# A new data layout for a fused attention and spectral-gate kernel: whole-batch loads, doubled head blocks, one merged tail of frequencies

## The chip, the cores and the metric

The kernel runs on one core of a Trainium2 chip. The metric is the device time of one launch in microseconds (us). TensorE multiplies matrices; VectorE, ScalarE and GpSimd work on elements, and GpSimd also issues the loads that cast. "Clock" is the share of full speed that the throttle granted TensorE; 1.00 is full.

The record calls an execution slow when it is over 1.5% above the fastest of its kernel. All profiles after the first were taken in fast runs. The profile before was not: its execution, 414.37 us, is 2.0% above the fastest. Where this matters, the profile of run b_tt2 stands beside it (the same kernel but for four buffers in the gate; 409.01 us, fast). The span of a profile is about 2 us shorter than the time of the same execution.

## The reference, cut to what matters

Eight batches. In each, eight heads attend twice: 32 packed rows `p` attend to the keys and values, then the queries attend to the 32 packed results. The 512 columns so made go through a projection to `x1, x2, x3`; `x2` is filtered in the frequency domain, the three are multiplied, and an output matrix follows.

```python
p_packed = sm_attn(p, k, v)              # q, k, v: 8 batches x 8 heads x 576 x 64
out      = sm_attn(q, p_packed, p_packed)
x        = out.transpose(0, 2, 1, 3).reshape(B, S, H * D)
x1, x2, x3 = split(x @ w_proj, 3)        # 512 columns each
x2_conv  = irfft(rfft(x2) * rfft(filter))   # over the 576 rows
y        = (x1 * x2_conv * x3) @ w_out
```

The kernel keeps `out` as a product: the normalised weights of the second attention (`a2n`, 576 x 256) times a small matrix (`qm`, 256 x 1536: packed results times `w_proj`). So the Fourier transform is applied to `a2n`, and the spectrum, its product with the filter and the inverse follow.

## The kernel before

One batch passes through attention, then the gate of the batch before it. Every head has its own load of `k`, `q` and `v`, in rows of 64 values, cast to 16 bits on the way by the queue that GpSimd feeds:

```python
def att_stage1(b):
    for g in range(NPAIR):                       # values, one load per head
        for hh in range(2):
            nc.gpsimd.dma_start(v_ring[:, rv, :, 0:D],
                vflat[base:base + NT * P, :].rearrange("(i tl) d -> tl i d", tl=P))
    for g in range(NPAIR):                       # pairs of heads
        ...                                      # p: load, transpose, two copies
        for ti, (tensor_f, nm) in enumerate(((kflat, "k"), (qflat, "q"))):
            for hh in range(2):
                nc.gpsimd.dma_start(stt[:, :, hh, :], tensor_f[base:base + NT * P, :]...)
            # 5 transposes, 2 copies
        # 5 score matmuls, 2 exponentials
```

Normalising the second attention took 20 small multiplies per batch on VectorE (160 of them in the trace). The spectral product works on frequency tiles of 128, 128 and 33; the third costs as much as a full one (0.68 us a multiply against 0.69, 1.27 us each on GpSimd for both):

```python
for m in range(3):                               # 128, 128, 33 frequencies
    # fre, fim: spectrum of this tile (4 matmuls)
    nc.vector.tensor_tensor(out=tt1, in0=fre, in1=hre_sb[.., m, :], op=ALU.mult)
    nc.vector.tensor_tensor(out=tt2, in0=fim, in1=him_sb[.., m, :], op=ALU.mult)
    nc.vector.tensor_tensor(out=tt3, in0=fre, in1=him_sb[.., m, :], op=ALU.mult)
    nc.vector.tensor_tensor(out=tt4, in0=fim, in1=hre_sb[.., m, :], op=ALU.mult)
    nc.gpsimd.tensor_tensor(out=outre, in0=tt1, in1=tt2, op=ALU.subtract)
    nc.gpsimd.tensor_tensor(out=outim, in0=tt3, in1=tt4, op=ALU.add)
```

Program order: loads and keys of batch 0, weights, filter, rest of batch 0; then attention of batch b, gate of batch b-1. In the trace TensorE's matmuls follow this order.

The softmax here doesn't subtract the row's maximum and nothing guards it: scores larger than these inputs give would overflow.

## Time and profile before

| | before |
|---|---|
| median time | 408.25 us (406.24 to 414.37, 4 runs) |
| start, to the first key transposes of batch 1 | 70.4 us |
| first period | 47.9 us |
| steady period (mean of six) | 44.4 us: attention 24.0, gate 20.2 |
| last gate, last store | 24.0 and 4.2 us |
| busy: TensorE, VectorE, GpSimd | 333.9, 240.6, 228.2 of 412.6 us |

Read it by stages: the shares over the whole run hide that the start is short of data, that attention runs at a clock of 0.72, and that the gate waits for a product made on VectorE and GpSimd. The profiled execution was the slowest of its four (414.37 us). In the profile of b_tt2 the steady period is the same (44.3 us), but the start is 66.0 us and the first period 47.4. The lines themselves are in the prediction.

### The profile page before, as it was taken

How to read it: one execution, taken by the hardware profiler on the slowest of the kernel's cores; microseconds unless marked ns; L12 is line 12 of the kernel's file. 1: busy time of each engine (PE TensorE's matmuls, PEld its weight loads, DVE VectorE, ACT ScalarE, POOL GpSimd, SP SyncE). 2: the span in 40 equal slices, each digit the busy share in tenths (PEclk: the TensorE clock that was granted, in tenths of full speed). 3: DMA queues.
4: the chain of work that ended last, by engine and by line, in shares of the span. 5: the costliest groups of instructions: out<-in, count | busy, mean ns of one | idle time of the engine just before them, and what ended most of it. 6: DMA issues, size and time to landing. Idle time of an engine off the chain costs nothing.

```text
span 412.6 us, 6577 instructions
## 1 busy us (share of the span) xinstructions
PE 333.9 (81%) x2220; PEld 186.6 (45%) x2220; DVE 240.6 (58%) x832; ACT 159.9 (39%) x436; POOL 228.2 (55%) x247
## 2 busy tenths in 40 slices
PE   0365798768897979798998899798979798889985
PEld 0242214434554446544563365436544366436452
DVE  2246116474856485667656584748555855758382
ACT  1011137345253715271346325452527143632323
POOL 8868301993449571996189536956397704043160
PEclk9999958659995899669985989588967997599999
DMA  9999901994069902991199409980499026000303
GB/s 200 182 208 210 227 2 10 87 86 26 1 141 103 71 1 105 108 95 7 53 138 97 30 2 162 98 55 2 127 106 81 2 76 75 0 2 0 116 0 116
DMA packets 138226, 33.05 MB, mean 80 GB/s; under 512 B 129552, under 2 KB 130960, under 8 KB 138192
## 3 DMA queue, kind: packets, MB, share of 16 engines
q0 software_dynamic: 125808, 15.72, 61.1%
q1 hardware_dynamic: 8096, 10.06, 7.4%
q10 hardware_dynamic: 4288, 6.85, 5.7%
q8 instruction: 17, 0.28, 0.3%
q14 instruction: 17, 0.14, 0.1%
HBM read 38.88 MB, written 9.44 MB: 117 GB/s over the span
## 4 chain that ended last, share of the span: by engine, by line
PE 50%; POOL 10%; DVE 9%; DMA 5%; issue 4%; POOLq 0%; ACT 0%; ACTq 0%; DVEq 0%
PE ops_b L392 9%; PE qps_b_g L298 8%; PE x2c_b L370 7%; PE fa2ps_b L318 6%; POOL gfull_b L350 5%; PE s_b_g L262 4%; DVE tt_b L341 4%; PE misc_b_g L253 3%; DMA qst_b_g<-in_q_dram 3%; DVE zrec_b_g L256 3%; PE x_b L376 2%; PE x_b L374 2%; PE trps_b_g L227 2%; PE a2tp_b L309 2%; POOL gtail_b L350 2%
## 5 line engine op out<-in xcount | busy, mean ns | idle before, releaser
L222 POOL DMA_DIRECT2D kst_b_g<-in_k_dram x63 | 55.5, 888 | 70.4 <-PE misc_b_g L207 53.2
L198 POOL DMA_DIRECT2D v_ring<-in_v_dram x63 | 55.4, 886 | 27.1 <-PE misc_b_g L253 24.9
L379 ACT COPY x1sb_b<-x_b 128x288 f32<-128x288 f32 x64 | 25.6, 399 | 98.3 <-PE x_b L374 70.4
L350 POOL TENSOR_TENSOR gfull_b<-tt_b,tt_b 128x512 f16<-128x512 f32 x16 | 20.3, 1268 | 69.6 <-DVE tt_b L341 69.6
L222 POOL DMA_DIRECT2D qst_b_g<-in_q_dram x63 | 55.7, 892 | 1.3 <-DMA v_ring<-in_v_dram 1.3
L370 PE MATMUL x2c_b<-afull_sb,gfull_b 128*128 128x288 f16 x256 | 45.7, 299 | 8.9 <-POOL gfull_b L350 8.7
L299 ACT CAST q_sb_b<-qps_b_g 64x512 f16<-64x512 f32 x96 | 49.4, 579 | 0.6
L298 PE MATMUL qps_b_g<-wp_sb,pp_ring 128*64 128x512 f16 x96 | 39.3, 594 | 0.0
L256 DVE RECIPROCAL zrec_b_g<-misc_b_g 64x32 f32<-64x32 f32 x64 | 19.5, 333 | 31.0 <-PE misc_b_g L253 30.8
L253 PE MATMUL misc_b_g<-e_b_g,v_ring 128*128 128x64 f16 (+1 forms) x320 | 32.5, 225 | 6.3 <-DVE pp_ring L257 4.7
L229 DVE COPY kT_b_g<-trps_b_g 128x512 f16<-128x512 f16 x32 | 13.6, 425 | 40.6 <-PE trps_b_g L227 39.3
L392 PE MATMUL ops_b<-wout_sb,yt_b 128*128 128x512 f16 (+1 forms) x160 | 36.8, 380 | 0.0
L340 DVE TENSOR_TENSOR tt_b<-fre_b,hre_sb 128x512 f32<-128x512 f32 (+1 forms) x24 | 16.5, 689 | 32.9 <-PE fre_b L333 29.7
L376 PE MATMUL x_b<-a2t_b,q_sb_b 128*128 128x288 f16 x128 | 32.6, 287 | 3.9 <-ACT x1sb_b L379 3.9
L370 PEld LDWEIGHTS <-gfull_b 128*128 128x128 f16 x256 | 24.7, 101 | 23.6 <-POOL gfull_b L350 15.5
L374 PE MATMUL x_b<-a2t_b,q_sb_b 128*128 128x288 f16 x128 | 31.5, 290 | 1.9 <-ACT x1sb_b L379 1.9
L262 PE MATMUL s_b_g<-pp_ring,qT_b_g 128*128 128x64 f16 (+1 forms) x160 | 18.0, 238 | 16.3 <-DVE pp_ring L257 16.3
L395 ACT ACTIVATE osb_b<-ops_b 128x512 f32<-128x512 f32 (+1 forms) x40 | 23.8, 596 | 17.6 <-PE ops_b L392 8.9
L382 DVE SCALAR_TENSOR_TENSOR yt_b<-wtmp_b,x2c_b 128x288 f16<-128x288 f32 x64 | 26.9, 451 | 6.3 <-PE x2c_b L370 5.5
L381 DVE TENSOR_TENSOR wtmp_b<-x1sb_b,x_b 128x288 f32<-128x288 f32 x64 | 27.6, 447 | 4.9 <-ACT x1sb_b L379 4.4
L237 ACT ACTIVATE e_b_g<-misc_b_g 128x256 f16<-128x256 f32 x32 | 12.3, 383 | 43.0 <-PE misc_b_g L234 43.0
L253 PEld LDWEIGHTS <-v_ring 128*128 128x128 f16 (+1 forms) x320 | 21.1, 111 | 15.0 <-issue 6.6
(73 smaller groups left out, 586.5 us busy)
## 6 DMA issues: line engine op xcount, KB each, us to landing
out_dram<-osb_b SPq DMA_DIRECT2D x32, 256.0 KB, 2.1
v_ring<-in_v_dram POOLq DMA_DIRECT2D x63, 80.0 KB, 3.3
kst_b_g<-in_k_dram POOLq DMA_DIRECT2D x63, 80.0 KB, 3.3
qst_b_g<-in_q_dram POOLq DMA_DIRECT2D x63, 80.0 KB, 3.4
wpst<-in_moe_w_proj_dram ACTq DMA_DIRECT2D x12, 256.0 KB, 5.3
wost<-in_moe_w_out_dram ACTq DMA_DIRECT2D x4, 256.0 KB, 4.6
fst<-in_moe_filter_fft_dram ACTq DMA_DIRECT2D x4, 256.0 KB, 6.0
out_dram<-osb_b SPq DMA_DIRECT2D x8, 128.0 KB, 2.6
```

What stands on the lines that cost most here:

```text
L198: nc.gpsimd.dma_start(v_ring[:, rv, :, 0:D], vflat[base:base + NT * P, :].rearrange("(i tl) d -> tl i d", tl=P))
L222: nc.gpsimd.dma_start(stt[:, :, hh, :], tensor_f[base:base + NT * P, :].rearrange("(i tl) d -> tl i d", tl=P))
L253: nc.tensor.matmul(ppz, v_ring[0:tsz[i], rv, i, :], e1[0:tsz[i], i, :], start=(i == 0), stop=(i == NT - 1))
L256: nc.vector.reciprocal(zrec[:], ppzp[D:D2, hh, hh * NPK:(hh + 1) * NPK])
L262: nc.tensor.matmul(s2ps[0:tsz[i], i, :], qT[:, i * P:i * P + tsz[i]], pp_ring[:, g, :], start=True, stop=True)
L298: nc.tensor.matmul(qps[:], pp_ring[:, g, :], wp_sb[:, g, ts(c, 512)], start=True, stop=True)
L299: nc.scalar.copy(out=q_sb[r0:r0 + 2 * NPK, g // 2, ts(c, 512)], in_=qps[:])
L350: nc.gpsimd.tensor_tensor(out=outre, in0=tt1[0:nf, :], in1=tt2[0:nf, :], op=ALU.subtract)
L370: nc.tensor.matmul(x2c[:], lhs, rhs, start=(j == 0), stop=(j == nk - 1))
L374: nc.tensor.matmul(x1[:], q_sb[:, ht, ts(m, P)], a2t_sb[ht][:, c0:c0 + cn], start=(ht == 0), stop=(ht == 1))
L376: nc.tensor.matmul(x3[:], q_sb[:, ht, ds(2 * DM + m * P, P)], a2t_sb[ht][:, c0:c0 + cn], start=(ht == 0), stop=(ht == 1))
L392: nc.tensor.matmul(ops[0:tsz[i], :], yt_sb[:, m, i * P:i * P + tsz[i]], wout_sb[:, m, :], start=(m == 0), stop=(m == ND - 1))
```

## The change

Its intent: fewer, longer transfers; fewer, larger instructions; a shorter spectral product. The diff, cut to its core (`...` marks cuts):

```diff
-            nc.gpsimd.dma_start(v_ring[:, rv, :, 0:D], vflat[...])            # 24 loads per batch
-                    nc.gpsimd.dma_start(stt[:, :, hh, :], tensor_f[...])
+        nc.gpsimd.dma_start(kn[:], k[b].rearrange("h (p i) d -> p h (i d)", i=KI))   # rows of 1.5 KB
+        nc.gpsimd.dma_start(vn[:], v[b].rearrange("h (p i) d -> p h (i d)", i=KI))
+        nc.gpsimd.dma_start(qn[:], q[b, :, 0:512, :].rearrange("h (p i) d -> p h (i d)", i=4))  # 1 KB
+        nc.gpsimd.dma_start(qt[0:32, :, :], tail[0])
+        nc.gpsimd.dma_start(qt[32:64, :, :], tail[1])
...
+    rings = [const.tile([P, H, 2 * NPK], FP16, ...)]      # doubled blocks: two heads side by side
+        for t in range(2):                                # p times v for four heads at once
+            for i in range(KI):
+                nc.tensor.matmul(pv[:, t, :], e1[:, i, ts(t, P)], vn[:, 4 * t:4 * t + 4, ts(i, D)], ...)
+                nc.tensor.matmul(z1[:, t:t + 1], e1[:, i, ts(t, P)], ones[0:KP, :], ...)
...
-                nc.vector.tensor_tensor(out=a2n[0:tsz[i], i, ...], in0=..., in1=zb, op=ALU.mult)   # x20
+            nc.gpsimd.tensor_tensor(out=a2n[0:n, i0:i0 + w, :]..., op=ALU.mult)                     # x3
...
+        for c in (1, 0, 2):                               # projection: pairs in two halves of the output
+            for t in range(2):
+                for u in range(2):
+                    nc.tensor.matmul(qp[u * D:(u + 1) * D, :], Rd[:, g, NPK:3 * NPK], wp[:, g, ts(c, DM)], ...)
...
-        for m in range(NFT):                              # 3 tiles, 4 multiplies and 2 sums each
+        for m in range(2):                                # 2 such tiles, temporaries with bufs=2
+        ft = spectrum(4)                                  # merged tail: one multiply
+        nc.vector.tensor_tensor(out=gm[:, 4, :], in0=ft[:], in1=htail[:], op=ALU.mult)
...
+    pack_p(0, 1, "a"); prologue_filter(); att1(0); ...    # filter first, forward transform in attention
```

The merged tail: the 33 frequencies left over lie in one tile of 128 rows, real parts twice and imaginary parts twice. One multiply with a filter tile laid out to match gives all four products, and the inverse matmuls form their sum and difference.

## The prediction

> **What bounds the kernel now.** I read the busy shares first, then the 40 slices, then the chain of waits in order of time, and last a table of stages whose borders I took from that chain.
>
> ```profile
> PE 333.9 (81%) x2220; PEld 186.6 (45%) x2220; DVE 240.6 (58%) x832; ACT 159.9 (39%) x436; POOL 228.2 (55%) x247
> ...
> PE   0365798768897979798998899798979798889985
> ...
> PEclk9999958659995899669985989588967997599999
> DMA  9999901994069902991199409980499026000303
> ...
> q0 software_dynamic: 125808, 15.72, 61.1%
> ```
>
> No engine is full. TensorE is the busiest, but its row dips at the start and, once per batch, its clock falls to half. The transfers saturate the first 50 us and then come in bursts. One queue carries nearly all of the cost: 15.72 MB in 125808 packets, 125 bytes each.
>
> The chain of waits ends each batch with the 20 output matmuls. Two of these, 118.27 and 162.47, are one steady period of 44.2 us apart. I cut that period where the spectrum matmuls begin:
>
> ```profile
> 0.00:70.40 70.40, 40.08 (x197) 17.50 (x197) 25.53 (x89) 16.30 (x44) 38.47 (x48) 0.90 1.22 152
> ...
> 118.30:142.30 24.00, 21.21 (x166) 12.63 (x166) 14.33 (x72) 13.42 (x41) 20.83 (x24) 0.72 1.38 108
> 142.30:162.50 20.20, 17.45 (x106) 9.70 (x105) 14.16 (x29) 5.92 (x13) 7.52 (x6) 1.00 0.09 34
> ```
>
> Columns: window, length, busy time and count of TensorE, its weight loads, VectorE, ScalarE, GpSimd, then clock, DMA share, GB/s. So there are four pieces: a prologue of 70.4 us (to the first key transposes of the second batch), seven periods (the first one 47.9 us, it still fills up; six of about 44.3), the gate stage of the last batch (24.0 us), and 4.2 us for the last store. Their sum is 412.6 us. Attention takes 24.0 us of a period at clock 0.72, the spectral gate 20.2 us at full clock.
>
> ```profile
> 133.43 4.71 PE qps_b_g L298 x12
> ...
> 150.16 1.20 POOL gtail_b L350
> 151.50 1.27 POOL gtail_b L351
> 152.82 0.66 PE x2c_b L370 x4
> ...
> 158.04 4.43 PE ops_b L392 x20
> ```
>
> From the chain: in attention the bound is TensorE's program order with short dependent steps at half clock (12 projection matmuls of 512 columns take 4.71 us, 0.39 each; the 20 output ones at full clock take 4.43, 0.22 each). In the gate it is the spectral product, VectorE then GpSimd, whose tail lands at 152.8, 10.5 us after the stage began. Loads appear on the chain, but in 118.3 to 125.9 the same table has TensorE busy 6.85 of 7.6 us with other heads, so that wait hides little.
>
> **What the Trainium skill says.**
> 1. "DMA: Bandwidth & Descriptors", Specifications: transfers under 512 B do not reach line rate. The trace agrees: 129552 of 138226 packets are under 512 B and they make up the saturated prologue. An engine's packet costs 0.611 x 412.6 x 16 / 125808 = 32 ns.
> 2. "TensorE: Matmul & The Clock Gate", Part 1: TensorE runs at half clock until it has been busy for a window of about 3.4 us, and falls back after an idle one. The trace agrees: clock 0.52 in 125.9 to 138.1, full again 4.9 us into the dense projection.
> 3. The same page, Part 3: matmuls whose outputs start in different column groups can run concurrently. No row of this trace has such a pair; the new projection does.
> 4. "VectorE: DVE Perf Modes", Two Vector instructions with no wait between them: an instruction whose operands start in another quadrant is held until the earlier one is done. Agrees: two reciprocals take 0.57 us, hardly less than twice one (0.33).
>
> **The change, part by part.**
>
> *Loads.* Per batch 24 loads become 5. Rows of 256 B in HBM become 1536 B (k, v), 1024 B (q) and 256 B (q tail). GpSimd spent 0.89 us on each old load, 24 x 0.89 = 21.3 us per batch. The new ones have 3072 rows; at 0.89 us per 640 rows that is 4.3 us. On the DMA engines the old rows cost 15360 x 32 ns / 16 = 31 us per batch. For the new ones I take 75 ns per 1.5 KB (estimate: the two hardware queues, with mean packets of 1.2 and 1.6 KB, took 60 and 88 ns per packet by the same division), 55 ns per 1 KB, 32 ns for the tail: (1536 x 75 + 1024 x 55 + 512 x 32) / 16 = 11.7 us. In steady state neither was on the path for long; this pays in the prologue.
>
> *Prologue.* The order of instructions puts the filter first, before any attention; its 2 MB now come on two uncontended hardware queues in rows of 4 to 6 KB. Filter and constants landed: about 9 us. 50 filter matmuls of 512 columns: 9 cold at 0.43 (spacing seen at 40 us) and 41 at 0.2165 (spacing seen at 43 us), 12.8 us, plus 5 x 0.2 us for the 64-row tile (20 old forward matmuls of 289 columns took 3.31 us where 0.122 each makes 2.44: 0.2 more for each of four groups that end in 64 rows): 23 us. Attention of batch 0, from the steps below, 25 us, plus 28 transposes for the rest of p (0.10 each, cold) and their copies, about 4: 52 us. Constants, load 0, the rest of p (1792 rows x 32 ns / 16), weights (1536 x 80 / 16) and load 1 need about 9 + 11.7 + 3.6 + 7.7 + 11.7 = 44 us of DMA, so they just keep ahead. Against 70.4 and the slow first period (47.9 - 44.3 = 3.6): **22 us saved**.
>
> *Attention of a period*, on TensorE in the order that the build gives. Old: 24.0.
> - Keys: per pair of heads 6 transposes (0.50, from 4 in 0.40), copy (VectorE 0.46, ScalarE 0.65: old 512 columns 0.43 and 0.58 scaled), 6 score matmuls (0.33), handovers 0.08. The next pair's transposes stand behind these scores, so nothing overlaps: 1.5 us warm, 1.9 cold; four pairs with the first 5 us warm and ScalarE's exponentials in front of its copies: 6.5.
> - p times v: 12 matmuls of 256 columns and 12 of one column, cold: 12 x 0.213 + 12 x 0.10 = 3.8.
> - Normalisation: drain 0.2, reciprocal 0.2, four multiplies in four quadrants, held, 4 x 0.29: 1.65. Nothing stands in TensorE's order in front of the transposes that wait for it.
> - Transposes of p and q (24 x 0.10) and two copies of 1024 columns (0.70 each), then 20 score matmuls: 4.4.
> - Projection: 12 x 0.427 cold = 5.1, or half if the pairs overlap. But the normalised weights go over GpSimd, 1.27 us for 512 columns: exp 0.6, reduce 0.64, reciprocal 0.2, then 1.27 + 1.27 + 0.7, ready 4.2 us after the scores end. So overlap saves under 2 us.
> - Forward transform 10 x 0.2165 + 0.4, tail 10 x 0.06 + 0.4, transposes 0.95: 4.5.
> Sum 6.5 + 3.8 + 1.65 + 4.4 + 5.1 + 4.5 = 26.0 serial, 24.3 overlapped; I take **25.0, one more than before**. Some 56 small VectorE instructions per batch vanish (40 multiplies of 0.21 us among them), but they ran beside TensorE and pay nothing here.
>
> *Gate.* The merged tail replaces four multiplies of 0.68 by one and two GpSimd operations of 1.27 by none; doubled temporaries remove the 0.2 us stalls. First multiply at 1.07 us, eight at 0.605: end 6.0; GpSimd's four end at 7.45 instead of 10.5. Fewer inverse matmuls fit ahead of it (about 17 of 72 instead of 31, as banks are freed by those multiplies): 55 x 0.122 = 6.7, then 4.43: **18.6 instead of 20.2**.
>
> Period: 25.0 + 18.6 = 43.6 against 44.3, so 7 x 0.7 = 5 us. The last gate does not repeat the forward transform: 18.6 against 24.0, but that work is only moved into the prologue's 52. Total 52 + 7 x 43.6 + 18.6 + 4.2 = 380 us in a profiled run; times 409.05 / 412.6: **377 us**.
>
> **The rivals.**
> - *TensorE stays warm through attention.* Then the steps fall to about 21 us (keys 6.2, p times v 2.0, projection hidden by GpSimd): 7 x 4 = 28 us less, 350. For it: fewer switches to 64-row tiles, a denser p times v. Against: the old attention was busy 21.2 of 24 us by this count and still fell to 0.52; the new one has longer gaps.
> - *The undivided key, normalisation and query steps cost more than I allow*, as all heads now wait together where the old order filled one pair's wait with another pair's transposes. Attention 28: 398 us, about 3% faster. For it: the program order, and every new copy being larger. Against: fewer instructions.
> - *The prologue is bound by casting transfers.* If long rows cost as much per byte as the short ones (32 ns per 256 B), each load takes 28 us and the weights 24: prologue near 90, total 415, slower. Against: the 2 KB rows above, and 32 ns looks like a cost per packet.
> - *GpSimd becomes the bound*: 4.3 + 3.2 + 5.1 = 13 us per period: no.
>
> **Range and chances.** Steps of attention are uncertain by 2 us, times 7, the prologue by 6, the gate by 1, times 8: together about 18. I take 353 to 398 for 8 in 10. The limit of 2% is 401 us; only the second rival at its worst or the third one reach it: faster 0.90, same 0.07, slower 0.03.
>
> **What would show it.** The first key transposes of the second batch near 52 us; DMA share of the software queue near 20 to 25%; output matmuls 43.6 us apart; the window of attention near 25 us with a clock still near 0.7; the last spectral product on GpSimd about 7.5 us after the spectrum begins; gate 18.6. Wrong it would be if periods are under 40 (warm clock) or over 46 (serial steps), or if the prologue does not shrink.

## The result, and the profile after

| | before | predicted | after |
|---|---|---|---|
| time | 408.25 us | 377 (353 to 398) | 357.59 us (356.74 to 358.35, 4 runs) |
| start | 70.4 | 52 | 53.3 |
| first period | 47.9 | 43.6 | 41.4 |
| steady period | 44.4 | 43.6 | 39.9 |
| attention / gate | 24.0 / 20.2 | 25.0 / 18.6 | 21.6 / 18.0 |
| last gate / store | 24.0 / 4.2 | 18.6 / 4.2 | 17.9 / 3.7 |

The ratio is 0.875 (95% interval 0.870 to 0.879): the changed kernel is faster. The record notes no check of its result, but calls runs that leave its arithmetic alone (a_short, a_serialproj) correct. The periods are the distances between the starts of the output matmuls of neighbouring batches. Of the 56.8 us between the two profiled spans, the start gives 17.1, the first period 6.5, the six steady ones 26.7 and the end 6.6. Against the fast profile of b_tt2 (span 407.0) they are 12.7, 6.0, 26.5 and 6.0: some 4.4 us of the 17.1 are the slow execution, not the change.

The page of the changed kernel: busy times, then 40 slices of the span (TensorE, its clock, transfers), then the software queue (packets, MB, share).

```profile
PE 281.9 (79%) x2162; PEld 170.7 (48%) x2162; DVE 161.6 (45%) x376; ACT 127.1 (36%) x259; POOL 94.7 (27%) x106
...
PE   0596777789868896789777896789778896889995
...
PEclk9997675699958998599959998699968997599999
DMA  7999961940369004920378014930300012000303
...
q0 software_dynamic: 29408, 16.52, 35.2%
```

TensorE lost 52 us of busy time, VectorE 79 and GpSimd 134, yet the row of the clock still has one dip per batch, as before. The packets fell to less than a quarter, the share of the queue only to 35.2%: a packet now costs 0.352 x 355.8 x 16 / 29408 = 68 ns instead of 32.

The same table of stages as in the prediction: start, one attention, one gate.

```profile
0.00:53.30 53.30, 33.47 (x240) 16.92 (x240) 15.58 (x35) 15.98 (x29) 18.53 (x28) 0.86 1.16 196
...
134.50:156.10 21.60, 16.54 (x160) 10.82 (x159) 6.78 (x19) 9.36 (x19) 6.25 (x8) 0.76 0.72 108
156.10:174.10 18.00, 16.58 (x106) 9.62 (x106) 12.31 (x27) 5.57 (x12) 4.95 (x4) 1.00 0.11 38
```

Attention has TensorE busy 16.5 of 21.6 us at clock 0.76; the gate is at full clock. The chain of waits, in order of time, for the start and for one period (start, length, what):

```profile
1.26 10.56 DMA pnat<-in_p_dram
...
13.69 13.52 PE hp L204 x49
...
135.48 0.47 PE s_b L226 x6
...
135.97 0.49 ACT e_b L228
136.46 0.54 ACT kT_b L222
...
143.19 0.28 DVE ppn_b L245
...
151.18 1.05 POOL a2n_b L295
...
152.28 2.25 PE fp_b L320 x8
...
160.74 1.23 POOL gm_b L359
...
170.11 3.96 PE o_b L396 x17
```

In the start, a small load of `p` lands at 11.86 us and the filter's matmuls follow; they end at 27.2. In a period the chain hops in the key stage from the scores (`s_b`) to ScalarE's exponential and copy of the next keys (`kT_b`), goes through VectorE's normalisation (`ppn_b`), GpSimd's weights (`a2n_b`), the transform (`fp_b`), GpSimd's product (`gm_b`) and the output matmuls (`o_b`). So TensorE's dependent steps still set attention; no load is on the path of a period.

### The profile page after: what moved, and what is told of

Read it like the earlier page. It is cut to its first block, busy times and chain, and to the rows that moved or that the text cites. A ratio compares the mean times of both kernels' runs of the same rounds, so it can differ in the third digit from the quotient of the medians.

```text
span 355.8 us, 5499 instructions
## 1 busy us (share of the span) xinstructions
PE 281.9 (79%) x2162; PEld 170.7 (48%) x2162; DVE 161.6 (45%) x376; ACT 127.1 (36%) x259; POOL 94.7 (27%) x106
## 3 DMA queue, kind: packets, MB, share of 16 engines
q0 software_dynamic: 29408, 16.52, 35.2%
q10 hardware_dynamic: 288, 1.56, 1.1%
## 4 chain that ended last, share of the span: by engine, by line
PE 61%; DVE 14%; POOL 11%; ACT 6%; issue 3%; DMA 3%; POOLq 0%; DVEq 0%; ACTq 0%
PE x_b L381 11%; PE o_b L396 10%; PE pv_b L235 6%; POOL gm_b L359 6%; PE fp_b L320 5%; PE s_b L226 5%; PE hp L204 4%; PE qTp_b L268 4%; DVE zs_b L291 3%; DMA pnat<-in_p_dram 3%; POOL gm_b L360 3%; PE x_b L378 3%; PE x_b L376 3%; DVE ppn_b L245 3%; ACT kT_b L222 3%
## 5 line engine op out<-in xcount | busy, mean ns | idle before, releaser
L381 PE MATMUL x_b<-ac,gm_b 128*128 128x288 f16 x320 | 51.2, 287 | 6.1 <-POOL gm_b L359 5.0
L383 ACT COPY x1s_b<-x_b 128x288 f32<-128x288 f32 x64 | 25.5, 398 | 80.0 <-PE x_b L376 59.8
L381 PEld LDWEIGHTS <-gm_b 128*128 128x128 f16 x320 | 30.0, 98 | 19.9 <-POOL gm_b L359 10.9
L396 PE MATMUL o_b<-wout,y_b 128*128 128x512 f16 (+1 forms) x160 | 38.2, 381 | 0.3
L226 PE MATMUL s_b<-pk,kT_b 128*96 128x64 f16 x192 | 17.1, 232 | 21.9 <-ACT kT_b L222 13.0
L320 PE MATMUL fp_b<-wc,a2n_b 128*128 128x512 f16 (+1 forms) x80 | 24.0, 400 | 11.7 <-ACT qm_b L309 8.5
L398 ACT ACTIVATE os_b<-o_b 128x512 f32<-128x512 f32 (+1 forms) x40 | 23.8, 596 | 22.1 <-PE o_b L396 22.1
L386 DVE SCALAR_TENSOR_TENSOR y_b<-w_b,x_b 128x288 f16<-128x288 f32 x64 | 26.8, 449 | 7.2 <-PE x_b L381 5.5
L385 DVE TENSOR_TENSOR w_b<-x1s_b,x_b 128x288 f32<-128x288 f32 x64 | 27.4, 448 | 4.5 <-ACT x1s_b L383 3.8
L378 PE MATMUL x_b<-a2t_b,qm_b 128*128 128x288 f16 x128 | 26.1, 286 | 3.9 <-ACT x1s_b L383 3.9
L376 PE MATMUL x_b<-a2t_b,qm_b 128*128 128x288 f16 x128 | 26.1, 286 | 1.0
L309 ACT CAST qm_b<-qp_b 128x512 f16<-128x512 f32 x48 | 24.0, 606 | 0.0
```

The source lines that it names most:

```text
L226: nc.tensor.matmul(s1[:, hh, 2 * ii:2 * ii + 2, :], kT[:, hh, ii, :], pk[:, b, 2 * g + hh, :], start=True, stop=True)
L309: nc.scalar.copy(out=qm[:, t, ts(c, DM)], in_=qp[:])
L320: nc.tensor.matmul(fp[:], a2n[0:n, i, ts(t, P)], wc[0:n, i, 0:DM], start=(i == 0), stop=(i == 4))
L376: nc.tensor.matmul(x1[:], qm[:, t, ts(m, P)], a2t[:, t, cols], start=(t == 0), stop=(t == 1))
L378: nc.tensor.matmul(x3[:], qm[:, t, ds(2 * DM + m * P, P)], a2t[:, t, cols], start=(t == 0), stop=(t == 1))
L381: nc.tensor.matmul(x2[:], gm[:, j, ts(m, P)], ac[:, j, cols], start=(j == 0), stop=(j == 4))
```

## The experiments

All were run against the kernel before; each was timed in three rounds. The edits are cut to what matters. Periods are means of six, from the profiles. "Start" is to the first output matmuls of batch 0 (113.7 us before, 89.9 after), or to the key transposes of batch 1 where said (70.4 and 53.3).

### Does the new layout pay through its rows? (no_load, short rows, one load per head)

**Before, loads of batches 1 to 7 removed.**

```diff
-        for g in range(NPAIR):            # loads of k, q, v
+        for g in range(NPAIR if b == 0 else 0):   # batch 0 only, its tiles are kept
```

> The kernel before, but keys, queries and values are loaded for batch 0 only and used again by the other seven batches (wrong result on purpose); TensorE's work is unchanged and the 21 us of descriptor writing per batch on GpSimd are gone. Theory of the prediction (old loads cost the start and the first period, and hide in the steady periods): steady periods stay at 43.5 to 44.5 us, the start shrinks by at most some 5 us because batch 1 no longer queues up behind the rest, total 395 to 408 us. Rival (the old loads also held up the steady attention, which is where its 2.4 us per batch were lost, and the new layout won by being easier on the DMA engines): attention falls by 2 us or more per batch, periods near 42 us, total 380 to 392 us.

Measured 394.99 us (before in these rounds 410.01), ratio 0.959 (0.950 to 0.969), wrong result. The steady period is 43.2 us instead of 44.4, the start 100.5 instead of 113.7. The loads were worth 1.2 us per batch, a bit more than allowed for and less than the rival needs. The start by its profile fell by 13 us, against 5 expected; but 7 x 1.2 = 8.4 of the 15.0 us between the medians leave only 6.6 for it, and the run with two temporaries (below) shows the old start scattering by 5 us with no cause. Against that run's fast profile the first outputs came 8.1 us sooner, and the keys of batch 1 at 58.7 instead of 66.0. What in the loads costs the 1.2 us stays open: the last steady period of the old kernel, with 6 loads left of 24, is no shorter than the others (44.56 us; 44.36 in b_tt2).

**After, keys and values in rows of 256 B.**

```diff
-        nc.gpsimd.dma_start(kn[:], k[b].rearrange("h (p i) d -> p h (i d)", i=KI))
+        nc.gpsimd.dma_start(kn.rearrange("p h (i d) -> p h i d", d=D), k[b].rearrange("h (i p) d -> p h i d", i=KI))
```

> The changed kernel with keys and values loaded in rows of 256 B instead of 1536 B, still one load per tensor and batch, same result. Packets of the software queue go from 29 to about 90 thousand. Theory (the row length is what pays in the start): DMA work per batch rises from some 12 to about 25 us, the second batch's key transposes move from 53 to 58 to 66 us, and since GpSimd must also write 9216 instead of 1536 rows per batch (some 3.6 us more of issue), the period grows by 0 to 2 us: total 363 to 382 us. Rival (the start shortened by order and fewer issues on GpSimd alone, row length does nothing): start within 1 us of 53.3, total within 3 us of 357.6.

Measured 354.77 us (354.03 to 355.10), correct. The queue's line of the page, and the group of key loads on GpSimd (count, busy, mean ns):

```profile
q0 software_dynamic: 90848, 16.52, 64.3%
...
L142 POOL DMA_DIRECT2D kn_b<-in_k_dram x8 | 14.3, 1792 | 76.9 <-PE kTp_b L217 73.2
```

Three times the packets and nearly twice the share of the DMA engines, and no time lost: batch 1's keys start at 51.5 us, the period is 39.95. The theory falls; the long rows of keys and values (1.5 KB) pay nothing here. The queries kept their rows of 1 KB in this run and the next, so those were not tested.

**After, the same short rows, one load per head.**

```diff
-        nc.gpsimd.dma_start(kn[:], ...)   # and vn, qn: 3 loads
+        for h in range(H):                # 24 loads
+            nc.gpsimd.dma_start(kn[:, h, :]..., k[b, h]...)
+            nc.gpsimd.dma_start(vn[:, h, :]..., v[b, h]...)
+            nc.gpsimd.dma_start(qn[:, h, :], q[b, h, 0:512, :]...)
```

> The changed kernel with keys and values in rows of 256 B and with one load per head, so 24 loads and two tails per batch as before the change, some 20 us of descriptor writing on GpSimd per batch instead of 3.6; same result. Rows of 256 B alone changed nothing, because the issue on GpSimd stayed short. Theory (the number of issues on GpSimd is what made the old start long): batch 1's key transposes move from 53 to 60 us or later, and the first output matmuls from 90 to over 97; steady periods 40 to 42 as GpSimd is free for only some 23 us before the next weights need it: total 365 to 385 us. Rival (the start is TensorE's program order, loads are early enough in any form): start within 2 us, periods as before, total within 4 us of 357.6.

Measured 385.42 us (383.17 to 387.56), correct: 30.7 us more than with the same rows of keys and values in whole-batch loads. Batch 1's keys start at 59.4, the first outputs at 102.4, the period is 42.8. Key loads on GpSimd, the chain in the start, and the wait that TensorE's list of instructions shows there:

```profile
L143 POOL DMA_DIRECT2D kn_b<-in_k_dram x64 | 48.1, 754 | 64.2 <-PE kTp_b L218 62.2
```

```profile
47.70 0.72 POOL vn_b L144
48.42 0.43 POOL qn_b L145
...
50.96 1.10 POOL a2n_b L296
...
52.10 4.93 PE fp_b L321 x10
```

```profile
52.10 4.93 PE L321 MATMUL fp_b<-wc,a2n_b 128*128 128x512 f16 x10 [7.75 <-POOL a2n_b L296]
```

GpSimd writes the loads of batch 1 from 27.5 to 50 us. Before 37.7 it stands 5.3 us in three places, by its list for transfers of the projection weights to land; from there on it writes without a pause. The weights of batch 0, which stand behind these loads in its order, come late; TensorE stands 7.75 us. The four steady periods in which such loads are issued take 43.4 to 45.1 us, the two after the last load 40.3 and 40.0, as in the changed kernel. So in this kernel the number of loads that GpSimd has to issue counts, not the rows of keys and values. A load of 576 rows holds GpSimd for 0.754 us, one of 4608 rows for 1.792: by these two, an estimate of 0.6 us per load and 0.26 ns per row. It gives 0.81 us for the changed kernel's key loads of 768 rows (0.805 measured), but 0.77 for the old ones of 640 (0.89 measured).

The 30.7 us are not the share of the gain that fewer loads brought. In the old kernel all loads of seven batches were worth 15.0 us; in the new one they cost more, because the normalised weights now wait behind them on GpSimd.

### The gate: doubled temporaries or merged tail?

**Before, two buffers for each temporary.**

```diff
-            tt1 = sbB.tile([P, DM], FP32, tag="tt1", ..., bufs=1)   # likewise tt2 to tt4
+            tt1 = sbB.tile([P, DM], FP32, tag="tt1", ..., bufs=2)
```

> The kernel before with two buffers instead of one for each of the four temporaries of the spectral product, nothing else. Theory: this is a small share of the gate's gain (the stalls of about 0.2 us at each of two reuses): 0.3 to 0.6 us per batch, total 403 to 407 us. Rival (the waits on the single temporaries were the main part of the gate's 2.2 us): 1.5 us or more per batch, total below 397 us.

Measured 407.92 us against 410.01, ratio 0.990 (0.980 to 1.000): not to be told from nothing. The period is 44.33 instead of 44.36. The whole of the 5 us between the two profiles lies ahead of the first output matmuls (108.7 against 113.7), where the edit does nothing: that is scatter of the old start. The theory's 0.3 to 0.6 us per batch is not there. VectorE's stalls did go (0.26 and 0.16 us in the batch of the prediction), and the last product came 0.4 us sooner after the first multiply, but the period did not follow.

**After, the cost of the unmerged tail put back.**

```diff
-        nc.vector.tensor_tensor(out=gm[:, 4, :], in0=ft[:], in1=htail[:], op=ALU.mult)
+        for j in range(4):
+            nc.vector.tensor_tensor(out=tt[j][:], in0=ft[:], in1=htail[:], op=ALU.mult)
+        nc.gpsimd.tensor_tensor(out=gm[0:64, 4, :], in0=tt[0][0:64, :], in1=tt[1][0:64, :], op=ALU.subtract)
+        nc.gpsimd.tensor_tensor(out=gm[64:128, 4, :], in0=tt[2][64:128, :], in1=tt[3][64:128, :], op=ALU.add)
```

> The changed kernel with the cost of the unmerged tail put back in the spectral product: four multiplies on VectorE and two operations on GpSimd for it instead of one multiply (wrong result on purpose). Two buffers for the temporaries did nothing in the kernel before, so the merged tail should be nearly the whole gain of the gate. Theory: three more multiplies of 0.69 and two more GpSimd operations of about 1.2 us at the end of the chain; the last product lands 3 us later, TensorE covers a part with other matmuls, the gate goes from 18.0 to about 20 us: total 370 to 376 us. Rival (the gate gained by its transposes and forward transform having left it, and the tail is covered): gate under 18.6, total under 362 us.

Measured 369.44 us (368.67 to 371.73), wrong result. The period is 41.8 instead of 39.9, a gate 19.8 instead of 18.0. TensorE's list shows the wait that came back, for the last product:

```profile
166.78 1.03 PE L385 MATMUL x_b<-ac,gm_b 128*128 128x288 f16 x7 [0.97 <-POOL gm_b L366]
```

The merged tail is 1.8 of the gate's 2.2 us, as the theory had it.

### The projection's pairs

**After, another order, so that neighbours mostly write the same half.**

```diff
-            for t in range(2):
-                for u in range(2):            # halves 0, 1, 0, 1, ...
+            for u in ((0, 1) if c != 0 else (1, 0)):
+                for t in range(2):            # halves 0, 0, 1, 1, 1, 1, 0, 0, ...
```

> The changed kernel with its 12 projection matmuls in another order, so that most neighbours write the same half of the output partitions and can't run beside each other; same instructions, same result. If neighbours in different halves do run concurrently (12 in 2.66 us at half clock, where 12 x 0.427 would be 5.1), they now take 4 to 5 us. As GpSimd's normalised weights arrive only 4.1 us after the projection begins, the period grows by 0.5 to 1.5 us and the total by 4 to 11 us, to 362 to 369 us. Rival (the short time comes from the trace's modelled ends, not from concurrency): no change in projection or total, within 1 us.

Measured 357.04 us (355.85 to 359.00), period 40.05, correct. A miss: at half clock a pair of these matmuls takes 0.43 us, against 0.42 in the order before, so the order of neighbours is not what makes them fast. (All 12 take 1.5 to 2.9 us in either kernel, by where the clock rises, so single batches can't be compared.) It did not show that they run side by side, nor that they don't.

**After, all 12 into one half.**

```diff
-                    nc.tensor.matmul(qp[u * D:(u + 1) * D, :], ...)
+                    nc.tensor.matmul(qp[0:D, :], ...)      # the copy takes qp[0:D] alone, qm is zeroed once
```

> The changed kernel with all 12 projection matmuls of a batch writing the lower half of the output partitions, one over the other (wrong result on purpose; the copies take that half alone). The run with another order left the pace as it was, 12 in 2.4 us, so order is not what makes them overlap; this one leaves no second column group to overlap with. Theory (two column groups work side by side, each through its own six): 12 now take 4.7 to 5.1 us at half clock instead of 2.8, the forward transform starts 1 to 2 us later, periods 40.7 to 41.7 us, total 363 to 371 us. Rival (64-column weights simply run at this pace, or the next wait hides it): projection under 3 us or period within 0.4 us of 39.9, total within 3 us of 357.6.

Measured 356.03 us (355.74 to 356.65), wrong result, period 40.15. TensorE's list, first the changed kernel's 11 (a twelfth starts 0.15 us earlier), then this run's 12:

```profile
148.23 2.66 PE L307 MATMUL qp_b<-wp,ppk 128*64 128x512 f16 x11
```

```profile
146.40 4.10 PE L310 MATMUL qp_b<-wp,ppk 128*64 128x512 f16 x12
```

Both parties were half right. Two halves do work side by side: by the starts in the trace, a pair takes 0.42 us at half clock and 0.22 at full with them, 0.86 and 0.43 without. And it pays nothing: in the changed kernel the transform behind the projection then waits for ScalarE's copies and GpSimd's weights, here for nothing. These are the changed kernel's two waits:

```profile
151.27 0.60 PE L320 MATMUL fp_b<-wc,a2n_b 128*128 128x512 f16 x2 [0.37 <-ACT qm_b L309]
152.28 2.25 PE L320 MATMUL fp_b<-wc,a2n_b 128*128 128x512 f16 x8 [0.41 <-POOL a2n_b L295]
```

From the first projection matmul to the end of these ten it takes 6.4 us, the run with one half 6.6.

### Attention's waits and the clock

**Weights normalised on VectorE instead of GpSimd.**

```diff
-            nc.gpsimd.tensor_tensor(out=a2n[0:n, i0:i0 + w, :]...
+            nc.vector.tensor_tensor(out=a2n[0:n, i0:i0 + w, :]...
```

> The changed kernel with the normalisation of the attention weights multiplied on VectorE instead of GpSimd. Same result. Theory (with overlapping projection pairs the transform waits for GpSimd, by 0.4 us, and otherwise for ScalarE's six copies of the projection): gains only about 0.4 us per batch, total 353 to 357 us. Rival (GpSimd sets the end of attention): the transform starts 1 us or more sooner, total 346 to 351 us.

Measured 346.99 us (345.54 to 348.28), correct; period 39.0, 0.9 less. Nearer to the rival: GpSimd, busy for 27% of the run, was on the path all the same, by the place of its work. Six periods give 5.4 of the 10.6 us; the rest lies ahead of the first outputs (84.9 against 89.9), and part of that may be scatter (the keys of batch 1 start at 50.1 here, at 53.3 in the changed kernel, but at 51.1 in a_tail6, which leaves everything before them alone).

**Query transposes ahead of the wait for the normalised heads.**

```diff
+        # in att1, in front of the normalisation: 20 query transposes, copies on ScalarE
-        # in att2: the same transposes, copies on VectorE
```

> The changed kernel with the transposes of the queries placed in TensorE's order before the wait of 1.5 us for the normalised packed heads, which they don't need; two of their copies go to ScalarE so that VectorE is free for the normalisation. Same result. Theory (that wait is idle time on the path): the transposes, 2.1 us at half clock, fill it; attention falls by 1 to 1.6 us and the total by 8 to 12 us, to 345 to 350 us. Rival (the later wait for GpSimd's normalised weights or the queue on ScalarE swallows it): total within 3 us of 357.6.

Measured 359.55 us (357.13 to 361.12), correct: nothing gained, the period is 40.9. TensorE's list behind the scores:

```profile
146.37 1.46 PE L308 MATMUL qp_b<-wp,ppk 128*64 128x512 f16 x11
149.50 0.61 PE L321 MATMUL fp_b<-wc,a2n_b 128*128 128x512 f16 x2 [1.67 <-POOL a2n_b L296]
150.51 3.54 PE L321 MATMUL fp_b<-wc,a2n_b 128*128 128x512 f16 x8 [0.40 <-POOL a2n_b L296]
```

The wait of 1.5 us was filled, the clock came back early and the projection ran at full speed (1.46 us instead of 2.66). Then TensorE stood 1.67 us for GpSimd's weights, the clock fell a second time, and the eight transform matmuls took 3.54 us instead of 2.25. The half clock had only moved to costlier work.

**Key transposes two pairs ahead of the scores.**

```diff
+        kTs = {g: keys(g) for g in range(2)}         # transposes and copy of two pairs
         for g in range(H // 2):
+            kT = kTs.pop(g)
             # 6 score matmuls of pair g
+            if g + 2 < H // 2:
+                kTs[g + 2] = keys(g + 2)
```

> The changed kernel with the key transposes running two pairs of heads ahead of the scores, so that TensorE doesn't stand for each copy. Same result. The prediction counted 'nothing overlaps' here; the trace shows four waits of 0.55 and 0.85 us, 2.8 us per batch. Theory (these waits are on the path): the first wait stays, the other three vanish or nearly: attention falls by 1.5 to 2.2 us, total by 12 to 17 us, to 341 to 346 us. Rival (ScalarE's exponentials and copies bound this stage, 1.2 us per pair of heads with a ScalarE copy): falls by under 0.8 us, total 351 to 356 us.

Measured 321.20 us (319.58 to 324.68), correct; period 35.8, 4.1 less. The clock over 40 slices, and the stages of one batch (attention, gate):

```profile
PEclk9999989799979999899979997899979997899999
```

```profile
118.80:136.40 17.60, 14.25 (x160) 9.28 (x160) 6.72 (x19) 9.36 (x19) 6.25 (x8) 0.90 0.86 134
136.40:154.30 17.90, 16.48 (x104) 9.53 (x104) 12.28 (x27) 5.58 (x12) 4.96 (x4) 1.00 0.10 37
```

The four waits of the key stage shrank from 2.8 to 0.64 us, as expected, but attention fell by 4.0. The other half goes with the clock: it now falls only behind the normalisation's wait, so p times v and its sums take 1.8 us instead of 2.8.

**Useless matmuls in the idle spots.**

```diff
+            fill(b, 2)     # behind each pair's key transposes: 512 columns each, result unused
+        fill(b, 6)         # in the normalisation's wait; 3 behind the query transposes,
+                           # 4 behind the projection
```

> The changed kernel with 21 useless matmuls of 512 columns per batch in TensorE's idle spots of attention (2 behind each pair's key transposes, 6 in the wait for the normalised heads, 3 behind the query transposes, 4 behind the projection); result unchanged. This is the first rival of the prediction, made to happen: if the idle spots are what sends the clock to half, the clock of attention rises from 0.76 to 0.95 or more; p times v falls from 2.75 to 1.4 us, queries and scores from 3.8 to about 2.5, with the fillers costing up to 1 us where they overrun their spots: total 340 to 356 us. Rival (the clock falls whatever TensorE does in this stretch): clock stays near 0.76, and the fillers only add, some 2 to 4 us per batch: total 370 us or more.

Measured 336.64 us (336.11 to 337.56), correct; period 37.7. The stages of one batch:

```profile
125.00:144.75 19.75, 17.42 (x180) 9.83 (x180) 6.68 (x19) 9.36 (x19) 6.24 (x8) 1.00 0.76 120
144.75:162.70 17.95, 16.52 (x104) 9.56 (x104) 12.32 (x27) 5.57 (x12) 4.96 (x4) 1.00 0.10 35
```

Twenty-one matmuls of 0.22 us more per batch made it 21 us faster. The clock is 1.00 throughout, p times v and its sums take 1.8 us. The rival falls: the idle spots are what sends the clock down.

**The three edits together.** Keys ahead, queries ahead, weights on VectorE.

> The changed kernel with three edits together: key transposes two pairs ahead (321.2 us alone), query transposes before the normalisation's wait (359.6 alone, because the half clock then came later, in the transform), normalised weights on VectorE (347.0 alone). Same result. Theory (what the wait costs is mostly the half clock that it causes, and with all three gone nothing sends it down): mean clock 0.97 or more, attention 15 to 15.5 us, periods 33 to 34, total 298 to 306 us. Rival (the wait for the weights behind the projection still sends the clock down and the transform runs cold, as in the run with the query transposes alone): mean clock under 0.95, total 312 to 325 us.

Measured 299.26 us (298.20 to 302.80), correct, ratio to before 0.730 (0.726 to 0.734): it beats both kernels. Stages of one batch:

```profile
109.10:124.30 15.20, 12.24 (x159) 8.44 (x158) 7.14 (x20) 11.28 (x21) 3.60 (x5) 1.00 1.00 156
124.30:142.20 17.90, 16.47 (x103) 9.51 (x102) 12.33 (x27) 5.57 (x12) 4.96 (x4) 1.00 0.10 35
```

Alone the edits were worth 36.4, 10.6 and -2.0 us, 45.0 in sum; together 58.3. That the query edit, useless while GpSimd's wait stood behind it, pays once the clock stays up is the likely reading, but it is not shown: the other two were not run without it.

The traces show one thing more about the clock. In every profile it changes only on a grid of 3.41 us (to 0.004 us; read from the clock's records in the packed traces). In the changed kernel each of the eight falls within the run comes after a grid step in which TensorE's list has it busy for 1.3 to 2.0 of the 3.41 us, each rise after one with at least 3.39. The grid does not move with the batches, so the same stage meets it at another place each time: in batches 2 to 7 the clock falls 3.7 to 5.9 us after the first key transposes. With this fits that the six steady periods of the changed kernel differ by 0.8 us (39.5 to 40.3) and those of the last run, where the clock stays up, by 0.1. A single batch is poor evidence where the clock changes.

## Why the prediction was right or wrong

The direction and the range held; the time was 19 us too high. In profiled spans it was 24 us (380 against 355.8), and nearly all of it, 6 x 3.7 = 22 us, is the steady period. The 380 were scaled down by a slow profile of the kernel before (409.05 / 412.6), which hid some 5 us of the miss.

**Start: right in size (52 against 53.3), wrong in cause.** The gain on it was put at 18.4 us with the slow profile; against the fast one it was 12.7. Its parts: the filter's matmuls began at 12.2 us instead of about 9, because the small load of `p` in front of them landed late; with 15 instead of 14 us they ended at 27.2 instead of 23; attention of batch 0 with the rest of `p` took 26.2 instead of 29. The 44 us of transfers that should "just keep ahead" were not near the path: with short rows their cost nearly doubled and the start did not grow. (The sign that went with it, a share of 20 to 25% for the software queue, came out at 35.2%: 29408 packets at 68 ns, where the loads alone had been counted, 24576 at a mean of 61.) The prediction put the gain on row length, and of GpSimd's 21.3 us of issue per batch and the 31 us of transfers it said that "neither was on the path for long". The run with one load per head shows the reverse for this layout: +7.9 us to batch 1's keys over the short rows alone, +2.9 us per period. The rival of the casting transfers was rightly rejected, though for a weaker reason than the runs give.

**Attention: the step that failed.** "25.0, one more than before" became 21.6. Term by term, in the batch shown:

| term | predicted | measured |
|---|---|---|
| keys | 6.5 | 5.65 |
| p times v and its sums | 3.8 | 2.8 |
| normalisation | 1.65 | 1.5 |
| p and q transposes, query scores | 4.4 | 3.8 |
| projection and forward transform | 9.6 serial, 7.9 overlapped | 7.9 |

Three assumptions carry some 2.6 of the 3.4 us; shorter transposes and scores (0.6) and normalisation (0.15) are the rest. The keys were to run half cold; here the clock stayed at 1.00 to their end (in other batches it fell sooner, and the keys took up to 6.2 us). The twelve one-column matmuls were sized at 0.10 us each and took 0.4 together. And of 26.0 serial and 24.3 overlapped I chose 25.0; the overlapped sum was the right one, though not through the pairs: with one half alone a pair took twice as long and the period hardly grew (40.15 against 39.92). Why the old attention lost 2.4 us is settled in part: its loads were worth 1.2 of the 4.4 us per period by the run without them, the rest is the sum of shorter steps and was not separated further.

**Gate: right.** 18.6 against 18.0; the last product at 7.45 us into the stage was seen at 7.1. The merged tail carried it; the doubled temporaries, which I had credited too, carried nothing.

**The first rival was the one to take seriously.** I argued against a warm clock with "the old attention was busy 21.2 of 24 us by this count and still fell to 0.52", that is, I took the clock for given. It did not stay up in the changed kernel (0.76), so the forecast of 350 for it does not apply; but the runs with the key transposes ahead and with useless matmuls show that a wait in this stage costs its own length and then the half clock behind it. I had also written that a period under 40 us would mean a warm clock: 39.9 came at 0.76, so that sign was ill chosen.

**GpSimd as the bound: right by the sum of busy time (13 us per period at most), too simple.** It was never full, yet moving 3 of its instructions gave 10.6 us, and giving it 21 more loads took 30.7.

**Slips in the working.** The multiplies that vanish are 20 per batch, not 40. The terms of the normalisation add up to 1.56, not 1.65. The clock was full again 4.35 us into the old projection (137.59), not 4.9, and what went before its fall at 123.94 was no idle window: TensorE was busy 3.11 of the 3.41 us. The two reciprocals do not bear on the rule about quadrants: both read and write the same ones, and the second starts 0.08 us before the first ends. The four multiplies of the new normalisation, each in another quadrant, do: each starts 0.01 us after the one before has ended, and with 0.28 to 0.30 us each the estimate held.

What stays open: what share of idling within a step of 3.41 us sends the clock down (steps with 1.8 us busy have also kept it, and in the kernel before it fell after steps that the list has busy for up to 3.3 us); how much of the start's gain is its new order (filter first), and what the doubled blocks are worth, since neither was undone alone; and the scatter of the old start, which makes some 5 of the 56.8 us between the two profiles uncertain (the new one scatters by about 2).

## What to carry to other kernels

Count what an engine must issue in order, not only the bytes and packets: here 21 more GpSimd loads per batch cost 30.7 us where three times the packets cost nothing. Judge a wait on TensorE by what the clock does behind it; filling it, even with useless matmuls, may pay more than its length, but only if no later wait takes its place. Sum the steps of a stage with the clock that each of them will see, and test which part of a wide change carries the gain before crediting its name.

## What the Trainium skill lacked or had wrong

- "TensorE: Matmul & The Clock Gate", Part 1, gives an idle window of about 3.4 us as what brings the half clock. Here it fell behind a key stage in which TensorE was busy 2.86 of 5.65 us and no single wait was longer than 0.85 us; and it stayed at 1.00 where TensorE was busy 12.24 of 15.2 us with waits up to 1.14 us. The length of the window is borne out (the clock changes on a grid of 3.41 us), its idleness is not. The page mentions that short idles between groups can make the clock swing, but gives no share of idling at which it falls.
- "DMA: Bandwidth & Descriptors", Anatomy of one DMA, describes the fixed cost of a load as completion latency, and descriptor writing as small. Its remark that many descriptors cost little is borne out (0.26 ns per row), but it lacks the time for which GpSimd itself is held: about 0.6 us per load (an estimate from 0.754 and 1.792 us), in order with its other work, which was worth 30.7 us here at 26 loads instead of 5 per batch.
- No page that I read says that matmuls in two halves of the output overlap in whatever order the halves are written: a pair took 0.43 us with the halves in runs of two and four, 0.42 alternating and 0.86 all in one half, each at half clock.
